# Dividing by the softmax sum ahead of the f16 split instead of behind the PV product, in a fused attention and two-MLP kernel

## The chip, the cores and the metric

The kernel runs on one core of one Trainium2 chip. The metric is the device time of one execution in microseconds. An execution is timed from outside, so its time is a little longer than the span between the first and the last instruction in the profile.

## What is computed

The input is q, k and v of 4 batches and 8 heads, 576 positions, 64 channels. For each head, the scores are `q k^T / 8`; scores lower than the row's maximum less `tau` are dropped; the rest goes through a softmax, whose denominator is the sum of the kept exponentials plus 1e-9; and the result multiplies v. The heads are laid side by side, which gives x of 2304 rows and 512 columns. The first MLP is `g(x @ w_in) @ w_out` with `g(h) = P(h) / Q(h)`, a cubic over a quadratic, and 2048 hidden columns. The second is `((x @ w1) * (x @ w2)) @ w3 @ w_out2` with 1024 columns. Everything is wanted in fp32.

## The kernel before

**Split numbers.** Most products run on f16 pairs: a number is written as hi + lo, and a product is three matmuls (hi hi, hi lo, lo hi). P and V are split too: the transposed P carries hi and lo in 9 blocks of 128 rows, V has 9 hi and 5 lo blocks, which gives the 14 steps of `pv` for each of two heads. Scores are fp32 matmuls. Weights arrive as 64-bit numbers. Three integer operations on VectorE (`conv_w`, L692, L695, L698) turn each tile of 128 x 512 into fp32, its squares give a scale, and `split_w` makes hi by a scaled copy and lo in PSUM by two products (L748 in fp32, L749) and a copy out. The product w3 w_out2 is formed once (`w_product`, L945).

**Attention.** One unit of work is (b, c, u): batch, pair of heads, and u = 0 for query blocks 0 and 1, u = 1 for blocks 2, 3 and 4 (block 4 holds 64 rows of both heads). For each block, `qk` makes scores of two heads in PSUM (tag S, two slots), `top` takes the row maximum on VectorE (L516), `thr` the threshold, and `exp` works in one of two ways: by ScalarE in two passes (L539, L544, the second summing rows into `su`), or by one pass of ScalarE (L537) and a select-and-sum on VectorE (L542). `p_hi` casts p to f16, `p_lo` subtracts, `p_t` transposes the pair by DMA (L596). Behind the last block of a unit, `recip` makes the reciprocals of 4 or 5 sums (L557, L558) and splits them into f16 hi and lo (L560, L561). `spread` multiplies them on TensorE with a small diagonal matrix `spot` (L574), so that the reciprocal of each query row stands along the free axis in PSUM; it is copied to SBUF (tile R). `pv` adds its 28 matmuls into the same PSUM bank (tag h), and `x_split` or `x_tail` multiplies that by R on VectorE (L620, L634), casts to f16 and subtracts.

**The order.** The kernel is written as a list of events (functions above, each a generator of one to five steps). A long constant string, ORDER, names for each step in turn the event's number, the engine where there is a choice (a, p or v: ScalarE, GpSimd, VectorE), and after dots the slots of the buffers that the step takes. The code issues the steps in that order, so the order within each engine's queue, and in the DMA queue of SyncE, is written out by hand. The first part of ORDER interleaves batch 0's attention with all weight work; after the last `split_w` come attention of batches 1 to 3, the first MLP (`h_product`, L824, and `y_product`, L888) and the second (`ab_product`, L995, and `o_product`, L1024).

**Setup.** Before all else `setup` issues three small loads (tau, and the coefficients a and b), fills constants on GpSimd, and works out a few scalars on ScalarE and VectorE.

Of the kernel before, what the change touches and what calls it, by code (L numbers as in the profile page):

```python
# [10 lines left out]
F32 = mybir.dt.float32  # L11
# [25 lines left out]
123.5 79v 53 125.4 102v.8 104p 123a 125a 156.0.1 36.6 106.1 127v.7 36 140.1 129p 159.0 36 43.7
30.0 161 43 131 163v.1 43 165.2.2 134v.5 167.8 165v 136p 59.2 167v 182.0.1 138 32.8 39.9 32 39 32
39 72.0 53 184.1 81.1 186 188p.2 190.4 175v.7 169p.3 53 177v 192.1 171v 190a 179.0 74.10 192a
219.0.1 55v.11 74 57.0 61.12 74 83a.2.2 221.2 62.0 80.1 61 83 80 61 116.1 207.2 99.2 223 66.0  # L40
64.13 225v.0 64 227.0.5 64 66 227v 76.0 232a.8 66 230.2 200p.7 202v 204 234v 230v 101.14 66 118.15
101 118 244.0.1 78.16 101 78 112.2 246.3 78 248 103.0 80 118 250p.1 252.1 215.5.7 85.1 194a.6
238p.0 240v 252a 196p 255.2 80 255a 105.17 105 263a.4 269.0 217p 82a.18 68v.19 107.1 281 105 265v
89.0 107 114.20 87.21 114 87 107 114 87 602.2 107 627.1 91.22 91 91 93.0 148.0 283.0.1 605.23 605
93 605 285.0 622.2 286 93 288a.2 290.1.2 150a.3.3 93 290a 150 624.24 608.0 630.25 624 95v.26 624
142.0 144 630 143.2 142v.1 630 610.27 128.1 610 173.1 146 610 594.0 146p 146v 166.0 242.2 594
130.28 145.29 130 594 109v.30 198 257a.3 130 145 613.1 259v 120.1 145 168.31 135.2 147.1 613 168
267 292.1 168 292a 613 299a.0 294v.6 151.0 295v 301p 613 304.0.1 615a.32 122.33 122 122 137.34
632.1 158.1 124.0 306.1 308 137 632 310p.0 314.2 137 314a 174.2 153.35 594 153 321a.1 277.7.4 153
323p 205.0 326.1 597a.36 126.0 328.2 312.5 632 132.0 330p.1 176.37 312a 160.38 176 133 632 155.0  # L50
160 176 160 189.2 635v.39 279p 181.1 157.1 206.40 139.0 315v.2 206 141 149 162.0 317v 178.1 164
206 170.0 191.41 212.0 149 355 172 180 191 110.0 191 180 220.2 183.42 183 183 214.43 197.1 185.1
214 187.0 214 209.1 211 222.44 228.0 209a.0 222 222 235.2 224.0 199.45 193.1 199 303.1 195 213 199
213a 70.1 229.46 213p 216.1 278.1 351.5.0 229 218.1 226 229 201.1 208.0 237.47 203 237 210 618.1
237 600.0 210 305.0 239.1 372.2 271.0 231.0 236.0 280.48 233 271a.1 280 241 353a 97.0 280 324 84.1
241 638.0 243 243 640 249v.49 256a.50 291.1 426.0 245p.0 253a.51 426 253.0 426 258v.52 272a.53
260a.54 274a.55 426 307.56 256.1 426 266p.0 251a.1 261 332.8 253v 332v 357.0.1 256a 307 339.1 307
247v.10 284.0 264v.12 268v.13 264.0 374.16 359.3 360 374 362a.2 273 364.2.1 374 366.3 287.14 311.2
364a 287 247.1 366a 287 275 264a 318.0 379.0.1 247v 275a 275v 251.0 380.0 373p.4 382 249.1 375p
251a 384a.0 260.0 249v 313.17 254a.21 276a.22 254.1 368v.3 260v 369p 254a 293.20 371.0 388.1 446.1  # L60
270v.23 293 388a 297.2 320.27 428.0 262a.3 293 320 428 331.1 313 386.3 320 270.0 313 430.0 325.0
338.2 386a 333p.6 432 272.1 319 270v 335p 400.1 432 272v 274.0 445 402.1 334.4 258.1 404a.1 274a
334 266.0 334 258a 365.1 446 266v 340.5 327.2 268.1 340 448.1 327 448.1 262.0 340 395a.8 450 430.0
358.2 397p 430.0 262v 450 406.7 337.2 346.0 348.1 346a.0 327 406a 435v 298.0 448.1 413.2 447.0.1
268a 377.2 452p 350 437 511.1 437 350p 449.2 455 350p 451 455 341.0 342 439.0 511 341a.1 344.0
361.24 344a 367.15 361 464.0 453v.2 344p 454.0.1 361 398 464 439 454a 367 352.2 439 457.1 513.0
367 457 345.1 515 458p.6 439p 515 457 441.0 316.0 343.0 460v 336.0 457v 462.1 322.0 347.6 300.8
296.1 347 363.0 354.25 347 309.1 354 378.1 349.0 407v.2 442.4.8 329.1 354 466.1 300 429.2 289.0
409p 468 468 411.1 456.6 456a 469.0.1 300 466.1 381.7 444v 356.0 389v.7 381 668.0 302.0 391p 370.0
282.0 471.3 393 376.0 472 466.0 381 474v.0 383.0 470v 425.1 478.0 385 385.0 473 385 482.0 478v  # L70
419a.9 387p.1 473 405v.29 390v.38 485a.3 421v.41 394a.33 392v.34 419.0 475.0 476.2 427.1.0 487p
476v 463a.7 390.1 433.1 419v 480p.0 410a.28 276.0 465p 390a 394.1 481p 276v 482 394v 483 475 392.0
# [1180 lines left out]
```

## Time and profile before

| what | value |
|---|---|
| median of 3 runs | 1107.4 us (1105.36 to 1110.74) |
| the profiled execution's own time | 1106.88 us |
| span in the profile | 1105.1 us |
| instructions | 16168 |
| TensorE busy | 997.3 us |
| VectorE busy | 869.7 us |
| ScalarE busy | 599.9 us |
| GpSimd busy | 330.9 us |

Busy time is the union of an engine's instructions: neighbours overlap a little at their ends, so a count times a mean is somewhat more than the busy time. Line numbers (L574) are those of the kernel before. PE is the matmul side of TensorE, PEld its weight load, DVE VectorE, ACT ScalarE, POOL GpSimd, SP SyncE; "SPq" is the DMA queue of SyncE.

### The profile page before, as it was taken

The page shows a single profiled execution, that of the slowest core. Times are in us where ns is not written, and L with a number is a line of the kernel's source. Part 1 is how long each engine was busy: PE and PEld are TensorE (multiplying, and loading weights), DVE is VectorE, ACT ScalarE, POOL GpSimd, SP SyncE. Part 2 cuts the span into 40 slices and gives each one's busy share as a digit, 9 for nine tenths or more (in the row PEclk, how much of TensorE's full clock was granted, in tenths as well). Part 3 has the DMA queues.
Part 4 walks back from the last instruction along what each step waited for, and adds up shares of the span by engine and source line. Part 5 has one row for each costly group of instructions (what it writes and reads, how often), then busy time and mean ns, then how long its engine had stood idle before and what let it go on. Part 6 is the DMA issues. An engine that isn't in the chain of part 4 may idle for free. (4 is left out here: it accounts for less than half of the span.)

```text
span 1105.1 us, 16168 instructions
## 1 busy us (share of the span) xinstructions
PE 997.3 (90%) x5599; PEld 480.3 (43%) x5604; DVE 869.7 (79%) x1756; ACT 599.9 (54%) x1118; POOL 330.9 (30%) x350
## 2 busy tenths in 40 slices
PE   3588769398789989999999999999999999999997
PEld 1334334143344445454444445454454454544443
DVE  5887888989897689889879977979778757775731
ACT  3341466777455377664677555885755434443430
POOL 2120213241131243342143354353233234321211
PEclk9889979698999999999999999999999999999999
DMA  8867787647675665768565678674675526622323
GB/s 235 218 206 210 218 208 200 175 99 192 146 196 148 129 118 115 166 131 186 110 136 116 148 140 169 134 174 85 146 146 97 112 47 132 114 58 48 58 48 86
DMA packets 334626, 154.70 MB, mean 140 GB/s; under 512 B 307408, under 2 KB 311504, under 8 KB 334544
## 3 DMA queue, kind: packets, MB, share of 16 engines
q1 hardware_dynamic: 334544, 153.67, 61.6%
q8 instruction: 44, 0.72, 0.3%
q14 instruction: 38, 0.31, 0.1%
HBM read 70.00 MB, written 8.13 MB: 71 GB/s over the span
## 5 line engine op out<-in xcount | busy, mean ns | idle before, releaser
L888 PE MATMUL y<-wp,gt 128*128 128x512 f16 x864 | 198.6, 379 | 1.7 <-DMA gt<-gg 1.1
L824 PE MATMUL h<-wp,xp 128*128 128x512 f16 x768 | 178.9, 381 | 5.0 <-DVE U L846 2.9
L349 POOL TENSOR_TENSOR hl<-p,hl 128x576 f16<-128x576 f32 x79 | 108.3, 1373 | 139.9 <-DVE hl L337 72.5
L507 PE MATMUL S<-raw 64*128 64x288 f32 x512 | 96.9, 458 | 47.8 <-ACT p L544 25.9
L995 PE MATMUL h<-wp,yy 128*128 128x512 f16 x576 | 132.6, 379 | 5.3 <-DVE R L634 1.9
L888 PEld LDWEIGHTS <-gt 128*128 128x128 f16 x864 | 82.5, 98 | 105.5 <-issue 6.9
L516 DVE TENSOR_REDUCE m<-S 128x1 f32<-128x576 f32 x144 | 104.4, 750 | 19.6 <-PE S L507 15.9
L824 PEld LDWEIGHTS <-xp 128*128 128x128 f16 x768 | 74.1, 98 | 99.2 <-issue 14.9
L1024 PE MATMUL y<-wp,gt 128*128 128x512 f16 x432 | 99.7, 379 | 0.8 <-DMA gt<-gg 0.8
L539 ACT ACTIVATE S<-S,th 128x576 f32<-128x576 f32 x97 | 67.7, 710 | 53.4 <-POOL th L356 33.7
L995 PEld LDWEIGHTS <-yy 128*128 128x128 f16 x624 | 59.4, 98 | 82.2 <-issue 12.0
L832 ACT ACTIVATE U<-h,cf 128x512 f32<-128x512 f32 x72 | 55.8, 777 | 67.1 <-PE h L824 42.4
L507 PEld LDWEIGHTS S<-raw 64*128 64x128 f32 x512 | 53.8, 198 | 88.1 <-ACT p L544 33.9
L349 POOL TENSOR_TENSOR A<-A,r 128x512 f32<-128x512 f32 x41 | 52.5, 1281 | 95.6 <-ACT r L839 95.5
L349 POOL TENSOR_TENSOR gg<-A,r 128x512 f16<-128x512 f32 x33 | 46.3, 1403 | 111.1 <-DVE A L867 76.8
L863 DVE SCALAR_TENSOR_TENSOR gg<-U,cf,r 128x512 f16<-128x512 f32 x72 | 59.1, 824 | 22.6 <-ACT r L856 15.6
L844 DVE SCALAR_TENSOR_TENSOR U<-h,cf,U 128x512 f32<-128x512 f32 x72 | 53.7, 746 | 28.1 <-ACT r L839 18.5
L544 ACT ACTIVATE p<-S,xy 128x576 f32<-128x576 f32 x97 | 71.6, 742 | 6.3 <-POOL hl L349 3.5
L748 PE MATMUL y<-cw,dg 128*128 128x512 f32 x112 | 64.1, 656 | 11.6 <-DVE gg L346 4.3
L945 PE MATMUL h<-cw 128*128 128x512 f32 x128 | 63.6, 652 | 6.5 <-DVE cw L698 2.9
L854 ACT ACTIVATE r<-A,lnb 128x512 f32<-128x512 f32 x72 | 51.8, 723 | 31.8 <-POOL A L349 23.8
L1024 PEld LDWEIGHTS <-gt 128*128 128x128 f16 x432 | 41.2, 98 | 52.1 <-issue 2.3
(199 smaller groups left out, 1697.3 us busy)
## 6 DMA issues: line engine op xcount, KB each, us to landing
rw<-in_moe_w_dram SPq DMA_DIRECT2D x32, 512.0 KB, 4.0
rw<-in_moe_w_out_dram SPq DMA_DIRECT2D x24, 512.0 KB, 4.6
raw<-in_k_dram SPq DMA_DIRECT2D x32, 288.0 KB, 3.3
wr<-in_v_dram SPq DMA_DIRECT2D x16, 576.0 KB, 4.9
rw<-in_moe_w_in_dram SPq DMA_DIRECT2D x16, 512.0 KB, 4.3
wr<-in_v_dram SPq DMA_DIRECT2D x16, 320.0 KB, 3.4
out_dram<-A SPq DMA_DIRECT2D x16, 256.0 KB, 2.5
d_y<-x SPq DMA_DIRECT2D x13, 256.0 KB, 2.3
```

Of the source, the lines that this page charges most:

```text
L349: (nc.gpsimd if eng[0] == "p" else nc.vector).tensor_tensor(o, x, y, op=op)
L507: nc.tensor.matmul(t[s][:, half, :HS], x[r, o:o + 128], y[r, keys], start=True, stop=True)
L516: nc.vector.tensor_reduce(st["m", b, c, blk][:, s:s + 1], t[:, :, :HS], axis=AX.XY, op=ALU.max, negate=True)
L539: nc.scalar.activation(t, t, AF.Prelu, bias=th, alpha=BIG)
L544: nc.scalar.activation(x, t, AF.Exp, bias=xy[:, 0:1], accum_out=su)
L748: nc.tensor.matmul(y, st["dg", dg], r, start=True, stop=False)
L824: nc.tensor.matmul(t, x[:, y, c, o:o + 128], w[:, a, :], start=c + i == 0, stop=c == KD - 1 and i == 2)
L863: stt(p[:, 0, :], u, cf[:, 3:4], r, ALU.add, ALU.mult)
L888: nc.tensor.matmul(st["y", n], x[:, 4 * a + j, :], w[:, y, :], start=f + j + i == 0, stop=f == 3 and j == 3 and i == 2)
L945: nc.tensor.matmul(t, st["cw", ("w3", m, j // 4)][:, o:o + 128], st["cw", ("wo2", j)], start=j == 0, stop=j == 7)
L995: nc.tensor.matmul(t, x[:, 4 * y + c, :], w[:, a, :], start=c + i == 0, stop=c == KD - 1 and i == 2)
L1024: nc.tensor.matmul(st["o", n], x[:, 4 * a + j, :], w[:, y, :], start=hf + j + i == 0, stop=hf == 1 and j == 3 and i == 2)
```

## The change

1. `recip` runs once for each block instead of once for each unit: (sum + 1e-9) x 2^-14 on any of three engines, then a reciprocal on VectorE. No f16 split of it. `spread`, `spot` and R go.
2. p is multiplied by the reciprocal ahead of its split. For head 0 of a block this is an extra pass over p in place (`p_norm`); for head 1 it is folded into the two steps of the split: `p_hi` gets a scale, and `p_lo` becomes one scalar-tensor-tensor operation, which only VectorE does in this code.
3. `x_split` and `x_tail` read PSUM directly: a copy scaled by 2^-14, and a scalar-tensor-tensor subtraction. The multiplication by R goes.
4. `setup` is cut into four events. `limits` (tau) and `powers` (a and b) hold the small loads, `diagonals` the two fills of 128 x 128. The new ORDER issues them as tokens 0, 1, 3, 2, then 6 (the first load of v).
5. ORDER is new throughout. The first loads are, before: tau, a, b, two weight tiles (512 KB each), v (320 KB), q, k; after: tau, a, b, two of v, one weight tile, q, k, and q, k of the next pair.
6. `su` has 8 buffers of 2 columns instead of 3 of 5; R and rr go.

Counted in the two ORDER strings, with the engine letters:

| step | whole order, before | whole order, after | up to the last split_w, before | up to the last split_w, after |
|---|---|---|---|---|
| exp, second step | 97 a, 47 v | 84 a, 60 v | 35 a, 11 v | 25 a, 21 v |
| recip | 32 of 4 VectorE instructions | 80: 40 a, 21 p, 19 v, and 80 reciprocals | 10 | 25: 14 a, 6 p, 5 v |
| p_norm | none | 36 a, 11 p, 33 v | none | 16 a, 2 p, 7 v |
| p_hi | 49 a, 33 p, 62 v | 66 a, 38 p, 40 v | 14 a, 12 p, 18 v | 20 a, 9 p, 13 v |
| p_lo | 79 p, 65 v | 47 p, 33 v, 64 fused on v | 23 p, 21 v | 15 p, 8 v, 19 fused on v |
| copy of spread to R | 26 a, 22 v | none | 8 a, 4 v | none |
| x_split, x_tail | 48 products, 96 further steps | 48 scaled copies, 48 subtractions | 12 units | 12 units |
| split_w, last copy | 34 a, 22 v | 23 a, 33 v | 34 a, 22 v | 23 a, 33 v |

Up to that point the new order also holds one more `qk` block and two more half steps of `ab_product`. The other events are the same, with some engine letters changed.

```diff
 ORDER = """
-0 45.0 49.1 1.2 12.0.1 47.0 47 47 3.0 51.1 51 51 2.0.0 13p 7.1 26.2 23.0.1 4.1 14.0 25.0 8.0 27
+0 1 3 2 6.0 4.1 49.2 15.0.1 22.2.3 5.0.0 7.1 53.1 29.0 51.0 51 16a 51 26.0.1 10.2 24a 28.0 30 55.1
...
-        R=2, m=4, th=3, su=3, rr=3, vs=2, sc=4, cf=6, xl=1,
+        m=4, th=3, su=8, vs=2, sc=4, cf=6, xl=1,
...
     def setup():
         nc.scalar.preload_act_table_set("natural_log_exp_and_others")
-        nc.sync.dma_start(out=tau_t, in_=tau.rearrange("(o c) -> o c", o=1).to_broadcast([128, 1]))
-        nc.sync.dma_start(out=pa, in_=ca.rearrange("(o c) -> o c", o=1).to_broadcast([128, 4]))
-        nc.sync.dma_start(out=bb, in_=cb.rearrange("(o c) -> o c", o=1).to_broadcast([128, 2]))
...
-        nc.gpsimd.memset(spot, 0.0)
-        nc.gpsimd.affine_select(out=spot, in_=spot, compare_op=ALU.not_equal, fill=2.0**-10,
-                                base=0, pattern=[[-1, 128]], channel_multiplier=1)
...
+        nc.vector.memset(xy[:, 1:2], 1e-9 * 2.0**-14)
+        nc.gpsimd.memset(qp, 0.0)
+
+    def limits():
+        nc.sync.dma_start(out=tau_t, in_=tau.rearrange("(o c) -> o c", o=1).to_broadcast([128, 1]))
...
-    def recip(b, c, u):
-
-        n = 5 if u else 4
-        su = st.pop(("su", b, c, u))[:, :n]
-        nc.vector.tensor_scalar(su, su, 1e-9, None, op0=ALU.add)
+    def recip(b, c, blk):
+
+        n = 2 if blk < 4 else 1
+        su = st["su", b, c, blk][:, :n]
+        small(su, su, 1e-9, 2.0**-14, xy[:, 1:2])
+        yield
         nc.vector.reciprocal(su, su)
-        t = st["rr", b, c, u] = T("rr", [128, 2, 5], F16)
-        nc.vector.tensor_scalar(t[:, 0, :n], su, 1024.0, None, op0=ALU.mult)
-        stt(t[:, 1, :n], su, 1024.0, t[:, 0, :n], ALU.mult, ALU.subtract)
-
-    def spread(b, c, u):
...
+
+    def p_norm(b, c, blk):
+        p = st["p", b, c, blk, 0]
+        copy(p, p, st["su", b, c, blk][:, 0:1])
 
     def p_hi(b, c, blk, s):
         hl = T("G", [128, 2 * S], F16, name="hl")
-        copy(hl[:, 0:S], st["p", b, c, blk, s])
+        copy(hl[:, 0:S], st["p", b, c, blk, s], st["su", b, c, blk][:, 1:2] if s else None)
         st["hl", b, c, blk, s] = hl
 
     def p_lo(b, c, blk, s):
-        hl = st["hl", b, c, blk, s]
-        rest(hl[:, S:2 * S], st.pop(("p", b, c, blk, s)), hl[:, 0:S])
+        hl, p = st["hl", b, c, blk, s], st.pop(("p", b, c, blk, s))
+        rest(hl[:, S:2 * S], p, hl[:, 0:S], st["su", b, c, blk][:, 1:2] if s else None)
...
-        t, y, p = st.pop(("pv", b, c, u)), st.pop(("R", b, c, u)), st["xp", b, u]
-        nc.vector.tensor_tensor(y, t[:, :256], y, op=ALU.mult)
-        yield
-        copy(p[:, 0, c, :], y)
-        yield
-        rest(p[:, 1, c, :], y, p[:, 0, c, :])
+        t, p = st.pop(("pv", b, c, u)), st["xp", b, u]
+        copy(p[:, 0, c, :], t[:, :256], 2.0**-14)
+        yield
+        rest(p[:, 1, c, :], t[:, :256], p[:, 0, c, :], 2.0**-14)
...
             for s in range(n):
                 at(exp, b, c, blk, s)
+            at(recip, b, c, blk)
+            at(p_norm, b, c, blk)
...
-    at(setup)
+    for fn in (setup, limits, diagonals, powers):
+        at(fn)
```

## Rows read from the trace of the kernel before

**Rows 1.** The page: clock granted to TensorE in 40 equal slices, in tenths.

```profile
PEclk9889979698999999999999999999999999999999
```

**Rows 2.** L337 by form: min/median/max ns, first and last start us.

```profile
L337 DVE CAST wp<-y x22: 676/684/693, 157.2 to 354.2; 128x512 f16<-128x512 f32 x22
...
L337 DVE CAST hl<-p x62: 446/454/1531, 24.6 to 946.1; 128x576 f16<-128x576 f32 x62
```

**Rows 3.** Windows, whole engines: us, busy (count), clock, DMA share, GB/s.

```profile
0.00:357.00 357.00, 269.57 (x1189) 126.81 (x1196) 299.91 (x645) 188.28 (x375) 83.34 (x98) 0.90 0.70 188
357.00:1105.00 748.00, 727.77 (x4414) 353.49 (x4410) 569.83 (x1111) 411.62 (x744) 247.55 (x252) 1.00 0.58 117
```

**Rows 4.** Waits, 28 to 357 us, SP's DMA queue: us, times, longest.

```profile
SPq L686 <- DVE cw L698: 62.4, 33, 4.9
```

**Rows 5.** The waits of PE in the same window.

```profile
PE S L507 <- ACT p L544: 21.2, 7, 13.2
```

**Rows 6.** Windows of L574 (spread): PE and PEld busy, clock, DMA share.

```profile
0.00:357.00 357.00, 4.97 (x80) 3.33 (x80) 0.90 0.70 188
357.00:1105.00 748.00, 12.89 (x240) 7.89 (x240) 1.00 0.58 117
```

**Rows 7.** The chain that ended last: start us, us, what.

```profile
788.52 1.29 PE h L824 x6
789.81 0.34 PE h L574 x8
790.16 1.53 PE h L611 x28
791.68 1.17 PE S L507 x8
```

**Rows 8.** Groups by form: busy us, mean ns of one, idle before, releasers.

```profile
L349 POOL TENSOR_TENSOR hl<-p,hl 128x576 f16<-128x576 f32 x79 | 108.3, 1373 | 139.9 <-DVE hl L337 72.5 <-ACT hl L333 58.6 <-issue 4.0
...
L349 DVE TENSOR_TENSOR hl<-p,hl 128x576 f16<-128x576 f32 x65 | 51.0, 784 | 5.0 <-ACT hl L333 2.1 <-POOL hl L337 1.9 <-DMA wr<-in_v_dram 0.8
...
L542 DVE SCALAR_TENSOR_TENSOR p<-S,th,p 128x576 f32<-128x576 f32 x47 | 37.6, 811 | 7.8 <-ACT p L537 7.3 <-POOL th L356 0.3
...
L346 DVE SCALAR_TENSOR_TENSOR vl<-wr,vs,vh 128x640 f16<-128x640 f32 x16 | 14.3, 904 | 2.3 <-ACT vh L335 2.3
...
L620 DVE TENSOR_TENSOR R<-h,R 128x256 f32<-128x256 f32 x32 | 13.4, 419 | 3.0 <-ACT R L333 2.3 <-PE h L611 0.7
...
L356 DVE TENSOR_SCALAR th<-m,c 128x2 f32<-128x2 f32 x24 | 6.5, 271 | 0.2
...
L339 POOL TENSOR_SCALAR wp<-cw,wsc 128x512 f16<-128x512 f32 x3 | 4.7, 1562 | 0.0
```

**Rows 9.** Window 0 to 357 us of L557 alone: DVE busy (count).

```profile
0.00:357.00 357.00, 3.23 (x10) 0.90 0.70 188
```

**Rows 10.** The same window of L561 alone.

```profile
0.00:357.00 357.00, 3.92 (x10) 0.90 0.70 188
```

**Rows 11.** The tile su: instructions of recip, min/median/max ns.

```profile
L557 DVE TENSOR_SCALAR su<-su x32: 153/170/1282, 24.9 to 947.7; 128x4 f32<-128x4 f32 x16, 128x5 f32<-128x5 f32 x16
L558 DVE RECIPROCAL su<-su x32: 177/184/192, 25.1 to 948.0; 128x4 f32<-128x4 f32 x16, 128x5 f32<-128x5 f32 x16
L560 DVE TENSOR_SCALAR rr<-su x32: 169/172/1199, 25.4 to 948.2; 128x4 f16<-128x4 f32 x16, 128x5 f16<-128x5 f32 x16
```

**Rows 12.** Windows, whole engines, two stretches dense in VectorE work.

```profile
414.00:552.00 138.00, 134.50 (x905) 67.49 (x904) 122.76 (x260) 86.16 (x164) 43.90 (x46) 1.00 0.68 142
552.00:690.00 138.00, 134.41 (x857) 66.52 (x855) 115.56 (x224) 85.69 (x158) 61.26 (x63) 1.00 0.70 142
```

**Rows 13.** Timeline of the start: start us, us, engine, line, idle before.

```profile
3.54 0.43 SPq L446 DMA_DIRECT2D raw<-in_q_dram  x1
...
7.38 0.42 DVE L692 TENSOR_SCALAR cw<-rw 128x512 int32<-128x512 int32 x1
...
9.91 1.20 POOL L339 TENSOR_SCALAR raw<-raw,flag 128x256 f32<-128x256 f32 x1 [7.29 <-DMA raw<-in_q_dram]
...
11.16 2.29 PE L507 MATMUL S<-raw 64*128 64x288 f32 x8 [11.16 <-POOL raw L339]
```

More of the change, by code (lines that the diff above doesn't have):

```diff
@@ L37 @@
[L37 to L48, printed above, removed]
@@ new lines @@
+1207a.7 1201v 1457.1 1083.1 1203a.1 1159 1295a.2.2 1204p 1218 1241.0 1091.0 1243 1206 1220v
+1245p.1 1091 1083 1209 1457 1083 1295 1210 1094.0 1066 1094.1 1083v 1160.1 1094.0 1461 1221p.5
+1452 1086.1 1247.1.8 1097 1099p 1247v 1461p.0 1229.1 1102 1097 1223p 1102 1113.0 1461p 1231v
+1224.0 1248.4 1248v 1231 1264.0.1 1250p 1464.0 1250 1105.1 1088 1252v 1266.1 1259p.1 1236.7.3
+1254a.2 1268 1088 1270v.0 1271.2.6 1466 1255p 1273.5 1271a 1113 1238p 1257.2 1273a 1105 1226.1
+1116.1 1275v 1261 1116.0 1300.0.1 1275 1116.1 1228v 1263.1 1105 1466 1162a.3.3 1228 1122p 1302.3
@@ L375, in tile_attention_mlps @@
     d1, b1, unit = c4[:, 0:1], c4[:, 1:2], c4[:, 2:3]
-    xy = cst.tile([128, 1], F32, name="xy")
+    xy = cst.tile([128, 2], F32, name="xy")
     ident = cst.tile([128, 128], F32, name="ident")
@@ L384, in tile_attention_mlps @@
     onesh = cst.tile([128, 128], BF16, name="onesh")
-    spot = cst.tile([128, 128], F16, name="spot")
     qp = cst.tile([128, 128], F32, name="qp")
@@ L413, in setup, with powers @@
                                     pattern=[[-1, 128]], channel_multiplier=1)
+    def powers():
+        nc.sync.dma_start(out=pa, in_=ca.rearrange("(o c) -> o c", o=1).to_broadcast([128, 4]))
+        nc.sync.dma_start(out=bb, in_=cb.rearrange("(o c) -> o c", o=1).to_broadcast([128, 2]))
         nc.scalar.activation(aa, pa, AF.Abs)
@@ L527, in exp @@
     def exp(b, c, blk, s):
-        u = min(blk // 2, 1)
-        if (u, s) == (0, 0) and blk == 0 or (blk, s) == (2, 0):
-            st["su", b, c, u] = T("su", [128, 5])
+        if s == 0:
+            st["su", b, c, blk] = T("su", [128, 2])
         p = T("G", [128, S], name="p")
-        x, k = p.rearrange("p (j c) -> p j c", j=2), 2 * (blk - 2 * u) + s
-        su, th = st["su", b, c, u][:, k:k + 1], st["th", b, c, blk][:, s:s + 1]
+        x = p.rearrange("p (j c) -> p j c", j=2)
+        su, th = st["su", b, c, blk][:, s:s + 1], st["th", b, c, blk][:, s:s + 1]
         t, m = st["S", b, c, blk][s][:, :, :HS], st["m", b, c, blk][:, s:s + 1]
@@ L628, in x_tail @@
     def x_tail(b, c):
-        t, y = st.pop(("pv", b, c, 2)), st.pop(("R", b, c, 2))
+        t = st.pop(("pv", b, c, 2))
         if b % 2 == 0 and c == 0:
@@ L633, in x_tail @@
         p = st["xl", b // 2][:, :, c, 64 * (b % 2):64 * (b % 2) + 64]
-        nc.vector.tensor_tensor(y, t[:, :64], y, op=ALU.mult)
+        copy(p[:, 0], t[:, :64], 2.0**-14)
         yield
-        copy(p[:, 0], y)
-        yield
-        rest(p[:, 1], y, p[:, 0])
+        rest(p[:, 1], t[:, :64], p[:, 0], 2.0**-14)
         if b % 2 and c == KD - 1:
@@ L657, in attention @@
                 at(p_t, b, c, blk, s)
-        at(recip, b, c, u)
         if u:
-            at(spread, b, c, 2)
             at(pv, b, c, 2)
             at(x_tail, b, c)
-        at(spread, b, c, u)
         at(pv, b, c, u)
```

487 lines of the change are left out of this document (241 added, 246 removed).

## The prediction

> **What bounds the kernel now.** I read the clock row of the page first: the slices in which TensorE is granted less than full speed all lie in the first quarter of the span [rows 1]. That suggests two regimes, and the last copy of a weight split, at 354 us [rows 2], shows where to cut. So the second view is the windows cut at 357 us [rows 3]. The reader should see that behind 357 us TensorE is busy 727.8 of 748 us at a granted clock of 1.00: this part is bound by matmuls, and 20 us is all that a better feed could give. Ahead of 357 us TensorE is busy only 269.6 us, at a mean clock of 0.90, while VectorE is busy 299.9 of 357 us, ScalarE 188.3 and GpSimd 83.3. VectorE is the fullest engine there, and the DMA queue confirms it: the weight loads wait 62.4 us in total for the last step of `conv_w` to free a buffer [rows 4]. It isn't a hard bound, because 57 us of VectorE stay idle; TensorE's own longest wait there is for the exponentials of the block before, which free PSUM for the next scores [rows 5]. I therefore price TensorE behind 357 us, and VectorE ahead of it.
>
> **TensorE's saving.** The L574 matmuls take 17.9 us of TensorE: 4.97 us ahead of the cut and 12.89 us behind it, 240 instructions for 12 pairs of heads [rows 6]. Behind the cut they lie on the chain that sets the end, 0.34 us for a group of eight, directly ahead of the 1.53 us of `pv` [rows 7]. Nothing hides them there, so all 12.9 us come off. The 4.97 us ahead of the cut lie where TensorE has 87 us idle; I don't count them as such. But the new order has, by the last weight split, one block of scores and two half steps of `ab_product` more behind it than the old one. On the chain a half step, six matmuls, takes 1.29 us and a block of scores 1.17 us [rows 7], so 3.7 us of later work are done in the early part in place of the spreads. What is left for TensorE behind the cut falls by 12.9 + 3.7 = 16.6 us. This assumes that the early part ends at the same time, which is the next step.
>
> **VectorE's early part.** Counts are those of the two orders up to the last `split_w`; durations are those of the rows. The select form of `exp` is used 10 times more: 10 x 0.811 = +8.1 us [rows 8]. The last copies of the weight split go from 22 to 33: 11 x 0.684 = +7.5 us [rows 2]. `p_lo`: 21 subtractions of 0.784 become 8 of them and 19 fused ones; the nearest fused operation is 0.904 us for 640 columns, or 0.81 for 576 [rows 8], together +5.2 us. `p_norm`: 7 passes. The trace shows no fp32 to fp32 pass of 576 columns; from below it is the cast at 0.454 us [rows 2], from above GpSimd's 1.56 us for 512 columns [rows 8]. On VectorE the cast is the nearer: +3.2 us. `p_hi` loses 5 casts: -2.3 us. `recip`: ten old ones took 3.23 us at L557 and 3.92 at L561 [rows 9, 10], and 10 x (0.184 + 0.172) at the two between [rows 11], 10.7 us; the new ones are 5 x 0.271 [rows 8] and 25 x 0.184 [rows 11], 6.0 us: -4.7 us. `x_split`, `x_tail` and the copies to R, 12 units: the product (0.419 for 256 columns [rows 8]) goes, as do four copies to R and nine further steps on VectorE; 12 subtractions and a copy come, each as long as the product, since they too read PSUM: about -4 us. Engine letters changed elsewhere take about 2.8 us off. The sum is +10 us of VectorE, on 300.
>
> How much of that reaches the end of the early part? Nothing, if it fits into the 57 idle us; 10 x 357/300 = 12 us, if the part keeps its ratio of busy time. VectorE waits little and is fed by loads that wait for it, so I'm nearer the second end: +7 us.
>
> **The part behind the cut, VectorE.** With the same prices on the whole order, the densest 100 us of TensorE in the old order carry 100 us of VectorE, and in the new one 104 us. Such a stretch measured 122.8 us of VectorE in 138, with TensorE still at 134.5 [rows 12], so the prices, which count overlapping ends twice, are about a tenth high, and four per cent more should still fit. ScalarE gets most of `p_norm` and has 52 of 138 us free there. I take +2 us, between 0 and +4. GpSimd has 94 us free in the same stretch: its 21 long scaled passes are hidden there by the distance between a block and its `pv`. If that cover were gone, each would cost its 1.56 us or more.
>
> **The start.** The constants don't in fact go behind the first loads: `limits` and `powers`, with their three DMAs, stand in the order ahead of the first load of v, as before. What moves is one weight tile, to behind v and q: 192 KB less ahead of q, which SP issued at 3.54 us and which GpSimd began to scale at 9.91; ScalarE now scales it, and the first matmul waited for that, at 11.16 us [rows 13]. In return the first `conv_w`, at 7.38 us, gets its tile later. Two pairs of q and k are now queued ahead of the second weight tile. Between -1.5 and +1 us; I take 0. The wait of recip's second step on its first, possibly on another engine, holds VectorE's queue at that place; what is queued behind are weight conversions and maxima, and it is in the 7 us above.
>
> **Sum.** 1106.9 (the profiled execution's own time) - 16.6 + 7 + 2 = 1099.3. That execution is 0.5 us below the median of the runs, well within their spread, so I forecast 1099 us.
>
> **A rule weighed.** VectorE's short tensor-scalar operations show a median of 0.170 us and a maximum of 1.28, while the reciprocal never exceeds 0.192 [rows 11]; the cast of p shows 0.454 and 1.53 [rows 2]. The Trainium skill, SBUF — State Buffer, section "Who interferes with whom", says that copies, casts and tensor-scalar operations on VectorE can take a port pair shared with GpSimd, and that the later of the two then stands still for the whole instruction of the other. The trace agrees in which instructions have the long tail. What it would do here is the last rival.
>
> **The rivals.**
> The early cost is hidden. VectorE's 10 us go into its idle 57, and the dense stretch costs nothing: 1106.9 - 16.6 - 1 = 1089. For it: TensorE's longest early waits are for exponentials [rows 5], which the normalization doesn't delay. Against it: the loads wait for VectorE [rows 4].
> Given back. The early part grows by the full 12 us, the dense stretch by 4 and the start by 1: 1106.9 - 16.6 + 17 = 1107. For it: VectorE is the fullest engine in both places.
> Slower. The normalization lengthens the way of each early block from its exponentials to its transposed P: threshold-sized step 0.27, reciprocal 0.18, `p_norm` 0.45 or more, 0.9 us at least, and about 1.2 with the waits between. If the early part is a chain through its 25 blocks rather than VectorE's sum, it grows by 30 us, and the time is 1106.9 - 16.6 + 30 + 2 = 1122. This decides from 0.66 us a block for no gain (16.6/25), and 0.9 for slower by half a per cent. Against it: scores wait for the exponentials alone, and the order keeps other work between a block and its `pv`.
> VectorE held. If each of the seven early `p_norm` passes on VectorE is held like the longest L557 (1.28 - 0.17 = 1.1 us), 7.8 us are added to the forecast: 1107. Against it: the median shows that most aren't held, and GpSimd has 32 fewer subtractions of 1.37 us [rows 8] to hold them with.
>
> **How the numbers follow.** Forecast 0.47, hidden 0.15, given back 0.15, slower 0.17, held 0.06. The forecast's own range is 1093 to 1105 (early part between +1 and +12, start and dense stretch at their ends in part). Half a per cent, 5.5 us, is about what a measurement of this kernel can tell from no change: faster is below 1101.9, slower above 1112.9. Of the forecast about 0.37 lies below 1101.9, and with the hidden case that is 0.52; 0.10 of it, given back and held make 0.31; slower 0.17. The range reaches from the hidden case's 1088 to 1113; the slower case is left outside.
>
> **What would show it.** No matmuls from a diagonal of 2^-10, TensorE's busy time lower by about 18 us; behind the last weight split TensorE 97% busy for some 731 us; that split's end at about 364 us, with VectorE busy about 310 us until then. If it ends near 357, the hidden case holds; if past 375, the slower one, and the scores' matmuls should then wait for more than the 21 us seen. If TensorE's idle time behind it is well above 20 us, the dense stretch was mis-sized. The forecast is wrong above all if the early part isn't ruled by VectorE's sum.

## The result, and the profile after

The changed kernel takes 1091.2 us, median of four runs (1090.44 to 1095.06), against 1109.07 for the kernel before in the same rounds: a ratio of 0.985, interval 0.981 to 0.989. A second, longer set of runs gave 1091.67 against 1106.94, 0.986 (0.984 to 0.989). The forecast of 1099 us was 8 us too long: the result lies below the forecast's own range (1093 to 1105) and only inside the wider one that takes in the hidden case, whose 1089 is nearer. Of the profiled executions, 1106.88 us became 1090.44: 16.4 us less, where 7.6 were forecast.

First the page of the changed kernel: busy time of each engine, and the clock granted in 40 slices.

```profile
PE 985.8 (91%) x5284; PEld 469.6 (43%) x5284; DVE 882.7 (81%) x1755; ACT 626.9 (58%) x1159; POOL 327.2 (30%) x325
...
PEclk9979979788999999999999999999999999999999
```

The low clock still stands in the first quarter alone, as in [rows 1]: the two parts are still there. The windows of the changed kernel at the same cut as [rows 3] (TensorE, its weight loads, VectorE, ScalarE, GpSimd, then clock, DMA share, GB/s):

```profile
0.00:357.00 357.00, 269.59 (x1137) 123.89 (x1138) 309.62 (x661) 197.87 (x384) 92.97 (x95) 0.91 0.71 189
357.00:1088.70 731.70, 716.20 (x4149) 345.73 (x4147) 573.12 (x1094) 429.03 (x776) 234.23 (x230) 1.00 0.60 119
```

Behind 357 us there are 731.7 us left, and VectorE is busy 309.6 us ahead of it: both are close to the figures that the prediction named (731 and 310). What it had wrong is where the last weight split ends. Its last copy starts at 352.8 us on ScalarE, the last on VectorE at 349.6, where the one before started at 354.2 [rows 2] and 364 was forecast. L336 and L340 are the new lines of the copies (minimum, median and maximum in ns, first and last start in us):

```profile
L336 ACT ACTIVATE wp<-y x23: 575/597/598, 153.2 to 352.8; 128x512 f16<-128x512 f32 x23
```

```profile
L340 DVE CAST wp<-y x33: 667/682/693, 155.3 to 349.6; 128x512 f16<-128x512 f32 x33
```

So from here on I cut each kernel at its own split: at the start of the last matmul that computes a split's remainder, 353.4 us before and 352.4 us after. The windows of the kernel before at that cut:

```profile
0.00:353.40 353.40, 265.97 (x1170) 125.06 (x1176) 298.38 (x642) 186.22 (x371) 80.46 (x96) 0.90 0.70 188
353.40:1105.10 751.70, 731.37 (x4430) 355.24 (x4428) 571.37 (x1115) 413.68 (x747) 250.43 (x255) 1.00 0.58 117
```

And those of the changed kernel:

```profile
0.00:352.40 352.40, 264.99 (x1115) 121.78 (x1116) 307.05 (x657) 194.34 (x377) 88.71 (x92) 0.91 0.72 191
352.40:1088.70 736.30, 720.80 (x4170) 347.84 (x4168) 575.70 (x1099) 432.57 (x782) 238.49 (x234) 1.00 0.60 119
```

The whole gain lies behind the split: 751.7 - 736.3 = 15.4 us, of which TensorE's busy time gives 731.4 - 720.8 = 10.6 and its idle time the rest (751.7 - 731.4 = 20.3 became 736.3 - 720.8 = 15.5). The early part is 1.0 us shorter, although VectorE does 8.7 us more in it. A second profile of the same kernel cuts elsewhere:

```profile
0.00:354.50 354.50, 264.32 (x1111) 121.58 (x1117) 307.09 (x657) 194.38 (x377) 88.50 (x92) 0.91 0.71 190
354.50:1089.20 734.70, 719.62 (x4170) 347.45 (x4168) 576.16 (x1099) 432.46 (x782) 238.41 (x234) 1.00 0.60 119
```

So 2 us of such a cut mean nothing, and the runs below show more scatter than that. Seven profiles of the new order with these 4170 matmuls behind the cut and no work added there have 718.6 to 721.2 us of TensorE behind it, in 732.0 to 736.6 us; two profiles of the old order with 4430 matmuls there have 731.4 and 735.6. Of the kernel before there is one profile only.

The waits of the early part (28 to 357 us, changed kernel), first the DMA queue, then TensorE: total, times, longest.

```profile
SPq L668 <- DVE cw L680: 67.9, 37, 4.5
```

```profile
PE S L506 <- DVE p L545: 13.4, 1, 13.4
PE h L696 <- ACT sq L687: 11.5, 7, 3.6
PE S L511 <- DVE p L545: 10.2, 4, 5.0
PE y L730 <- ACT wp L336: 7.2, 5, 2.7
PE S L511 <- ACT p L547: 5.5, 1, 5.5
```

The weight loads wait for VectorE a little longer than in [rows 4] (67.9 against 62.4 us), and the scores wait for the exponentials as in [rows 5]: 13.4 + 10.2 + 5.5 = 29.1 us, against 21.2 + 7.0 = 28.2 in the kernel before, whose second wait is for the exponentials that VectorE finishes:

```profile
PE S L507 <- DVE p L542: 7.0, 2, 6.5
```

None of TensorE's long waits is for a transposed P. What the normalization costs on each engine is shown by the tile of the sums:

```profile
L562 DVE RECIPROCAL su<-su x80: 147/156/167, 17.3 to 931.8; 128x2 f32<-128x2 f32 x64, 128x1 f32<-128x1 f32 x16
L349 DVE SCALAR_TENSOR_TENSOR hl<-p,su,hl x64: 790/810/1825, 18.3 to 928.2; 128x576 f16<-128x576 f32 x64
...
L338 ACT ACTIVATE p<-p,su x36: 759/775/800, 35.2 to 932.6; 128x576 f32<-128x576 f32 x36
...
L342 DVE TENSOR_SCALAR p<-p,su x33: 501/514/1161, 17.5 to 918.9; 128x576 f32<-128x576 f32 x33
...
L342 POOL TENSOR_SCALAR p<-p,su x11: 1723/1725/2811, 179.1 to 925.9; 128x576 f32<-128x576 f32 x11
```

One pass of `p_norm` is 0.514 us on VectorE (0.454 was assumed from the cast [rows 2]), 0.775 on ScalarE and 1.725 on GpSimd (medians). The fused subtraction is 0.810, as its nearest row, scaled to 576 columns, said [rows 8].

The start of the changed kernel:

```profile
3.54 0.44 SPq L450 DMA_DIRECT2D raw<-in_q_dram  x1
...
8.72 0.43 DVE L674 TENSOR_SCALAR cw<-rw 128x512 int32<-128x512 int32 x1 [1.53 <-DMA rw<-in_moe_w_dram]
...
9.06 0.51 ACT L338 ACTIVATE raw<-raw,flag 128x256 f32<-128x256 f32 x1
...
9.93 2.29 PE L511 MATMUL S<-raw 64*128 64x288 f32 x8 [9.93 <-DMA raw<-in_k_dram]
```

Against [rows 13], the first scores start 1.23 us sooner and the first `conv_w` 1.34 us later.

### The profile page after: what moved, and what is told of

It reads as the page before. It is cut to its first block, busy times and chain, and to the rows that moved or that the text cites. A ratio compares the mean times of both kernels' runs of the same rounds, so it can differ in the third digit from the quotient of the medians.

```text
span 1088.7 us, 15602 instructions
## 1 busy us (share of the span) xinstructions
PE 985.8 (91%) x5284; PEld 469.6 (43%) x5284; DVE 882.7 (81%) x1755; ACT 626.9 (58%) x1159; POOL 327.2 (30%) x325
## 5 line engine op out<-in xcount | busy, mean ns | idle before, releaser
L806 PEld LDWEIGHTS <-xp 128*128 128x128 f16 x768 | 74.5, 99 | 99.1 <-issue 15.5
L352 POOL TENSOR_TENSOR hl<-p,hl 128x576 f16<-128x576 f32 x47 | 66.8, 1421 | 108.5 <-ACT hl L336 58.3
L511 PEld LDWEIGHTS S<-raw 64*128 64x128 f32 x512 | 53.6, 198 | 75.4 <-issue 31.6
L730 PE MATMUL y<-cw,dg 128*128 128x512 f32 x112 | 66.7, 680 | 14.1 <-ACT wp L336 7.2
L826 DVE SCALAR_TENSOR_TENSOR U<-h,cf,U 128x512 f32<-128x512 f32 x72 | 53.4, 745 | 31.7 <-ACT r L821 18.7
L542 ACT ACTIVATE S<-S,th 128x576 f32<-128x576 f32 x84 | 58.1, 710 | 20.5 <-POOL th L359 13.1
L845 DVE SCALAR_TENSOR_TENSOR gg<-U,cf,r 128x512 f16<-128x512 f32 x72 | 54.2, 757 | 19.0 <-DMA gt<-gg 10.1
L547 ACT ACTIVATE p<-S,xy 128x576 f32<-128x576 f32 x84 | 62.1, 743 | 5.8 <-DMA pL<-hl 4.8
L927 PE MATMUL h<-cw 128*128 128x512 f32 x128 | 60.6, 626 | 2.5 <-ACT cw L336 1.4
```

Source lines behind the costliest of these rows:

```text
L352: (nc.gpsimd if eng[0] == "p" else nc.vector).tensor_tensor(o, x, y, op=op)
L511: nc.tensor.matmul(t[s][:, half, :HS], x[r, o:o + 128], y[r, keys], start=True, stop=True)
L542: nc.scalar.activation(t, t, AF.Prelu, bias=th, alpha=BIG)
L547: nc.scalar.activation(x, t, AF.Exp, bias=xy[:, 0:1], accum_out=su)
L730: nc.tensor.matmul(y, st["dg", dg], r, start=True, stop=False)
L806: nc.tensor.matmul(t, x[:, y, c, o:o + 128], w[:, a, :], start=c + i == 0, stop=c == KD - 1 and i == 2)
```

## The experiments

Two things were open: what the spread matmuls had really been worth (their recorded time, or less, by overlap), and why the early part did not grow (because VectorE's sum does not rule it, or because something was given back there). Ratios are to the kernel before in the same rounds; the changed kernel's own is 0.986. "Cut" is the last split, as above, and "behind" what lies from there to the end.

**The matmuls put back.** The new order, with matmuls of the number and shapes of the old spread ahead of each `pv`, from constants (of bf16, where the old ones were f16).

```diff
         vh, vl = st["v", b, c]
+        for i in range(2 if u < 2 else 1):
+            for a in range(2):
+                for h in range(2):
+                    ...
+                    nc.tensor.matmul(d, onesh[k, 0:64], onesh[k, k], start=a == 0, stop=a == 1)
```

> The changed kernel with the 320 small matmuls of spread put back on TensorE ahead of each pv: same shapes and count as before, operands constant, results in a part of the PSUM bank that nobody reads; all else as changed. Theory A (TensorE alone sets the time behind the last weight split, so the removed matmuls are the gain): slower than the changed kernel by 12.9 us, the busy time of these matmuls behind the cut in the kernel before, up to 16.5 with the gaps around them, which gives 1104 to 1108 us against a changed kernel of 1091. Theory B (the gain comes from the new order, not from the matmuls): slower by at most 5 us.

Measured: 1094.12 us, 0.9888 (0.9871 to 0.9904): by the ratios only some 3 us above the changed kernel. The windows of these matmuls alone (TensorE, weight loads) and of the whole:

```profile
356.90:1093.80 736.90, 12.88 (x240) 7.83 (x240) 1.00 0.60 119
```

```profile
356.90:1093.80 736.90, 724.30 (x4410) 353.29 (x4408) 572.27 (x1099) 432.48 (x782) 238.62 (x234) 1.00 0.60 119
```

By the record they are busy 12.88 us behind the cut, as before [rows 6]. TensorE's busy time rises by 3.5 us (720.8 to 724.3), its idle time falls by 2.9, and the part is 0.6 us longer, within the scatter of that part; the cut comes at 356.9, 2.4 to 4.5 later. A line's busy time is not what its presence costs. Part of it is overlap, which the timeline shows (start, us, what):

```profile
613.00 0.41 PE L600 MATMUL h<-onesh 128*64 128x128 bf16 x8
613.25 1.15 PE L606 MATMUL h<-pT,vh 128*64 128x256 f16 x18
```

A group of eight is recorded as 0.41 us, but `pv` starts 0.25 us after it did. So theory A is refuted for the matmuls by themselves.

**The matmuls taken out of the old order.** The kernel before, with no spread matmuls, and R filled with ones.

```diff
-        for i in range(2 if u < 2 else 1):
...
-                    nc.tensor.matmul(d, w.to_broadcast([k.stop - k.start, 64]), spot[k, k],
-                                     start=a == 0, stop=a == 1)
...
-        copy(y, t[:, n:2 * n])
+        copy(y, unit.to_broadcast([128, n]))
```

> The kernel before with its old order, but without the matmuls of spread; R is filled with ones by the same copies, so x isn't divided by the sums. Theory A: faster than before by 12.9 to 16.5 us, ratio 0.985 to 0.988, although order, setup and VectorE's work are the old ones. Theory B: at most 5 us faster, ratio 0.995 or more.

Measured: 1086.99 us, 0.9822 (0.9803 to 0.9841), 20 us less. Its windows:

```profile
0.00:345.60 345.60, 256.51 (x1091) 119.93 (x1096) 297.74 (x642) 185.19 (x370) 83.48 (x97) 0.92 0.72 192
345.60:1083.90 738.30, 721.70 (x4190) 349.19 (x4188) 571.22 (x1115) 413.00 (x748) 248.94 (x254) 1.00 0.59 119
```

Here the part behind the cut loses 751.7 - 738.3 = 13.4 us: 9.7 of TensorE's busy time and 3.7 of its idle time. And the early part, where VectorE does the same work as before (297.7 us), ends 7.8 us sooner. The time fell by more than theory A allowed, in the old order.

The two experiments differ in more than the order. The matmuls that I put back wait for nothing, and nobody waits for them; the old spread worked on the reciprocals, and its result was copied to R. In the kernel before, by its profile, these copies wait for `pv`, which writes the same PSUM bank, 16.1 us on VectorE and 20.7 on ScalarE in all (total, times, longest):

```profile
DVE R L337 <- PE h L611: 16.1, 14, 2.7
ACT R L333 <- PE h L611: 20.7, 11, 4.2
```

This run takes away these waits together with the matmuls, since its copies read a constant.

**The same in batch 0 alone.** The loop of the spread runs only where `b` is not 0, and R of batch 0 is filled with ones.

```diff
-        for i in range(2 if u < 2 else 1):
+        for i in range((2 if u < 2 else 1) if b else 0):
```

> The kernel before without the matmuls of spread in batch 0 alone (R is ones there, so batch 0 isn't divided by its sums); batches 1 to 3 as before. Without them everywhere the early part ended 7.8 us sooner and the rest took 13.4 us less. Theory E (the 4.97 us of spread ahead of the cut and the waits of TensorE in front of them, 3.0 us, lie on the path of the early part): the last weight split ends at about 346 us instead of 353, the rest is unchanged, and the time falls by 7 to 8 us. Theory F (TensorE's idle time takes the early spreads up; the earlier end had another reason): the split stays at 353 and the time falls by 2 us at most.

Measured: 1104.44 us, 0.9969 (0.9954 to 0.9985), 3.4 us less. Its windows:

```profile
0.00:347.00 347.00, 261.64 (x1095) 121.20 (x1096) 298.04 (x642) 185.39 (x370) 82.17 (x97) 0.91 0.71 191
347.00:1102.30 755.30, 735.61 (x4430) 356.63 (x4428) 571.32 (x1115) 414.20 (x748) 248.40 (x254) 0.99 0.58 117
```

The cut comes at 347.0, 6.4 us sooner, as theory E said, but the time falls by half of that: the part behind the cut is 3.6 us longer (755.3). So batch 0's 4.97 us of spread [rows 6], which lie where TensorE is idle a quarter of the time, do matter for the early end, with the waits and copies that go with them. Whether the other half is lost behind the cut or is scatter of single profiles (4.6 us in the new order) isn't shown; the times, with their interval, give 1.7 to 5.1 us.

**The matmuls put back elsewhere.** The same number, behind the scores of a pair's last block, into unused columns of S.

```diff
             st.pop(("qk", b, c, u))
+            for i in range(2 if blk == 1 else 3):
+                ...
+                        nc.tensor.matmul(d, onesh[k, 0:64], onesh[k, k], start=a == 0, stop=a == 1)
```

> The changed kernel with the same 320 dummy matmuls as in the run in which they stood directly ahead of pv, now directly behind the scores of a unit's last block, apart from pv, into unused columns of the scores' PSUM banks. Theory G (what such a group costs depends on its neighbour: beside pv, whose matmuls have the same size of stationary operand, 0.1 us a group; apart, 0.34 us): the part behind the cut is 8 to 10 us longer than in the changed kernel, against 0.6 us beside pv. Theory H (it doesn't depend on the place): 0.6 to 3 us longer, as beside pv.

Measured: 1096.74 us, 0.99 (0.9876 to 0.9923), by the ratios 4 us above the changed kernel. Behind the cut:

```profile
354.90:1095.50 740.60, 728.13 (x4386) 353.35 (x4384) 574.10 (x1098) 432.13 (x782) 239.56 (x234) 1.00 0.59 118
```

That is 4.3 us more than the changed kernel, between the two theories' figures, with 7.3 us more of TensorE's busy time. Of the added matmuls 216 lie there, recorded as 10.85 us, not 240. And the place brings waits of its own: VectorE's row maxima wait 9.1 us in the whole kernel for these matmuls, which stand in the scores' banks. So it isn't shown that the matmuls themselves cost more away from `pv`.

**Three sets of them.** As in the first experiment, three times.

```diff
+        for i in (0, 1) * 3 if u < 2 else (0,) * 3:
```

> The changed kernel with three times the matmuls of spread ahead of each pv (960, operands constant, nobody reads the results). One set, which on TensorE takes 0.21 us where eight stand together and 0.1 where four do, 6.3 us behind the cut, made the part behind the cut only 0.6 us longer and the kernel about 4 us slower. Theory J (TensorE is the bound behind the cut, but 3 us of its idle time there is slack that the first set used up): each further set comes in full, 12.6 us behind the cut and 3 us ahead of it, so 16 to 20 us slower than the changed kernel. Theory K (the small matmuls beside pv cost next to nothing): 4 to 8 us slower.

Measured: 1100.54 us, 0.9943 (0.9921 to 0.9966), 9 us above the changed kernel. Its windows behind the cut, of these matmuls and of the whole:

```profile
350.90:1096.70 745.80, 25.12 (x720) 20.07 (x720) 1.00 0.58 117
```

```profile
350.90:1096.70 745.80, 735.61 (x4890) 365.99 (x4888) 573.24 (x1099) 433.66 (x782) 237.35 (x234) 1.00 0.58 117
```

Against one set, two more add 735.6 - 724.3 = 11.3 us of busy time and 745.8 - 736.9 = 8.9 us behind the cut, 4.5 us a set. By the ratios, which rest on several runs each, one set costs 3.1 us and three cost 9.2: some 3 us a set, with no sign that the first is cheaper. That is nearer the lower expectation, and a quarter of the 12.9 us of the record. Ahead of the cut the three sets are busy 9.02 us by the record, and still the cut comes at 350.9, no later than the changed kernel's: the early part isn't lengthened by the matmuls' time as such. With one set it came at 356.9, so single cuts can differ by some 6 us for no reason that these runs show.

**VectorE's early load raised.** Two reductions of 512 columns, 0.68 us each, behind each reciprocal of batch 0: 40 in all.

```diff
         nc.vector.reciprocal(su, su)
+        for _ in range(2 if b == 0 else 0):
+            nc.vector.reduce_max(spare[:, 512:513], spare[:, 0:512], axis=AX.X)
```

> The changed kernel with two more reductions over 512 columns of a spare constant tile on VectorE behind each reciprocal of batch 0: 40 instructions of some 0.68 us, 27 us in all, in the early part where VectorE has 47 us idle. Theory C (VectorE's sum rules the early part): slower by 27 x 357/310 = 31 us. Theory A (idle time takes it up): slower by 5 us at most, with the last weight split within 5 us of its place.

Measured: 1105.81 us, 0.999 (0.9975 to 1.0005). Its early window:

```profile
0.00:371.00 371.00, 264.84 (x1110) 122.36 (x1116) 332.10 (x697) 194.51 (x377) 84.66 (x93) 0.90 0.68 181
```

25 us more of VectorE (332.1 against 307.1) move the cut by 16.5 to 18.6 us (to 371.0, from 354.5 or 352.4), and the time by 14: about 0.7 us for each us, the share of 7 in 10 that the forecast took. Neither theory's figure (31 and 5 us) was met.

**VectorE's early load lowered.** 24 early steps given to ScalarE by their letters in the order: the 7 `p_norm` and 17 last copies of `split_w`. The first and the last of them:

```diff
-... 40v ... 68v ... 929v ... 807v
+... 40a ... 68a ... 929a ... 807a
```

> The changed kernel with 24 steps of the early part moved from VectorE to ScalarE by their letters in the order: the 7 passes of p_norm (0.54 us each on VectorE, 0.77 on ScalarE) and 17 of the 33 last copies of the weight split (0.68 and 0.59). Takes 15 us off VectorE ahead of the cut and adds 15 us to ScalarE, which has 158 us idle there. Theory C (VectorE's sum reaches the early part's end with the slope of 0.69 that the run with more VectorE work showed): 10 us faster than the changed kernel. Theory I (ScalarE's queue then holds exponentials behind copies that wait for TensorE): 0 to 5 us faster, or slower.

Measured: 1090.91 us, 0.9845 (0.9817 to 0.9872). Its early window:

```profile
0.00:352.10 352.10, 261.78 (x1115) 120.53 (x1116) 295.05 (x633) 207.25 (x401) 86.78 (x91) 0.91 0.72 191
```

VectorE is 12.0 us shorter, ScalarE 12.9 longer, and the cut (352.1) and the time stay where they were. Theory C's 10 us are refuted for this move. It doesn't show that less work on VectorE is worth nothing, since ScalarE took the steps over: TensorE's waits for ScalarE's squares and copies of the weight split rise there from 11.5 + 7.2 = 18.7 us to

```profile
PE h L691 <- ACT sq L682: 13.8, 9, 3.6
PE y L725 <- ACT wp L331: 9.1, 8, 2.7
```

which is 22.9. Work moved to another engine isn't work taken away; no run takes early work off VectorE alone.

**No normalization.** `p_norm` does nothing; all other steps stay.

```diff
-        p = st["p", b, c, blk, 0]
-        copy(p, p, st["su", b, c, blk][:, 0:1])
+        pass
```

> The changed kernel without p_norm, so head 0 of each block isn't divided by its sum. Takes 36 passes off ScalarE, 11 off GpSimd and 33 off VectorE (17.9 us busy there), and one link from the way from exponentials to transposed P. Theory A (these passes are hidden in idle time): same as the changed kernel within 3 us. Theory C (VectorE's sum still rules the early part, as forecast): the early part ends about 4 us sooner (7 passes of 0.54 us on VectorE) and the time falls by 4 us. Theory D (the chain of each early block rules): 25 blocks by 0.5 us or more, 12 us faster.

Measured: 1086.34 us, 0.9828 (0.9806 to 0.9849): the 80 passes cost some 4 us, and the interval touches the changed kernel's. The cut comes at 349.8, against 352.4 and 354.5, with 2.9 us less of VectorE ahead of it and 11.3 less of ScalarE. Theory D is refuted; theories A (3 us) and C (4 us) can't be told apart. The new order without its normalization and the old order without its spread take the same time, 1086.3 and 1087.0.

**VectorE's load raised in the dense part.** One reduction behind each reciprocal of batches 1 to 3, 60 in all.

```diff
         nc.vector.reciprocal(su, su)
+        if b:
+            nc.vector.reduce_max(spare[:, 512:513], spare[:, 0:512], axis=AX.X)
```

> The changed kernel with one more reduction over 512 columns on VectorE behind each reciprocal of batches 1 to 3: 60 instructions of 0.66 us, 40 us of VectorE, nearly all behind the cut, where VectorE has 160 us idle. Theory J (TensorE alone bounds that part): 0 to 3 us slower. Theory L (the dense stretch from about 400 to 700 us, where VectorE is busy 90 per cent, is bound by VectorE too, as the 2 us of the forecast suppose): 6 to 15 us slower, with TensorE's idle time up in that stretch.

Measured: 1104.13 us, 0.9972 (0.9956 to 0.9988), 12 us above the changed kernel. Its part behind the cut, two stretches of it, and the same two of the changed kernel:

```profile
354.80:1104.00 749.20, 723.95 (x4170) 348.97 (x4168) 607.34 (x1155) 433.31 (x782) 237.40 (x235) 1.00 0.56 117
```

```profile
400.00:540.00 140.00, 131.56 (x828) 65.20 (x828) 128.28 (x260) 96.07 (x181) 56.23 (x51) 0.99 0.69 143
540.00:680.00 140.00, 135.59 (x771) 65.48 (x771) 128.08 (x244) 87.49 (x159) 51.12 (x50) 1.00 0.68 142
```

```profile
400.00:540.00 140.00, 135.56 (x859) 66.77 (x857) 127.05 (x257) 99.65 (x186) 59.62 (x53) 1.00 0.74 149
540.00:680.00 140.00, 139.29 (x833) 69.17 (x833) 123.90 (x252) 90.93 (x168) 55.09 (x56) 1.00 0.73 149
```

VectorE stays at 128 of 140 us, little above the 127 and 124 that the changed kernel has there; what gives way is TensorE, from 135.6 to 131.6 and from 139.3 to 135.6. Behind the cut VectorE has 31.6 us more, the part is 749.2 - 736.3 = 12.9 us longer, and TensorE's idle time in it rises from 15.5 to 25.3. So, as theory L has it, the dense part is not bound by TensorE alone: each us of VectorE costs 0.4. TensorE's busy time also rises by 3.2 us here, with not one matmul more: a rise of that size, such as the first set's 3.5, needn't be the added matmuls' own time.

**The constants really behind the loads.** In the order, the tokens of `limits` (1), `powers` (3) and `diagonals` (2) after the first loads.

```diff
-0 1 3 2 6.0 4.1 49.2 15.0.1 22.2.3 5.0.0 ...
+0 6.0 4.1 49.2 15.0.1 1 22.2.3 3 2 5.0.0 ...
```

> The changed kernel with the constants in fact behind the first loads: the two loads of v, the weight tile and the first q and k are issued first, then tau, then the second q and k, then the coefficients and the diagonals. Theory: the first three loads start 1.4 us sooner (three issues of 0.47 us less ahead of them), and tau, 1.7 us later in the queue, still lands ahead of q; the scores start 0.5 to 1.4 us sooner and the time falls by 0 to 1.5 us. Rival: the scaling of q waits for tau behind 1.1 MB of loads, and the time grows by 1 to 3 us.

Measured: 1095.39 us, 0.9877 (0.985 to 0.9904), not told apart from the changed kernel's 0.986. Its part behind the cut (735.0 us) and the cut itself (354.9) are those of the changed kernel. At the start it is the rival that came true: tau is used from 8.62 us on, where it was used from 3.31, and the first scores start 2.75 us later than the changed kernel's:

```profile
12.68 1.81 PE L511 MATMUL S<-raw 64*128 64x288 f32 x6 [12.68 <-ACT raw L338]
```

**Normalization folded into the split.** For the 33 blocks whose subtraction runs on VectorE, the sum's reciprocal is applied in the split of the first head instead of ahead of it; 14 `p_hi` go from GpSimd to ScalarE.

```diff
-        copy(hl[:, 0:S], st["p", b, c, blk, s], st["su", b, c, blk][:, 1:2] if s else None)
+        copy(hl[:, 0:S], st["p", b, c, blk, s], scale_of(b, c, blk, s))
...
-        rest(hl[:, S:2 * S], p, hl[:, 0:S], st["su", b, c, blk][:, 1:2] if s else None)
+        rest(hl[:, S:2 * S], p, hl[:, 0:S], scale_of(b, c, blk, s))
```

> A variant that computes the whole reference: in the 33 blocks in which VectorE does head 0's subtraction, the extra pass p_norm goes, and head 0 is scaled inside its split as head 1 is (a scaled p_hi, on ScalarE in 14 blocks where GpSimd cast it, and the fused subtraction). It takes 33 passes away: 15 on ScalarE (0.77 us), 12 on VectorE (0.54), 6 on GpSimd (1.96); it adds 0.05 to 0.1 us to each split step. Leaving all 80 passes out made the kernel some 3 us faster. Theory A (the passes are hidden): within 1 us of the changed kernel. Theory C: 1 to 3 us faster.

Measured: 1092.53 us, 0.986 (0.9833 to 0.9888): no gain. With at most 4 us to be had from all of `p_norm`, a third of it can't be seen.

**The changed kernel once more**, beside the last group of runs, for the cut's scatter.

> The changed kernel itself once more, beside the kernel before on the chip of this group of runs, so that differences of 3 to 6 us can be told: all theories expect a ratio of 0.982 to 0.988.

Measured: 1091.67 us, 0.9863 (0.9837 to 0.9889); cut 354.5, behind it 734.7 us, TensorE busy 719.6.

## Why the prediction was right, and which term was mis-sized

**In short.** The sign was right. The size wasn't: 15 to 18 us came off where 8 were forecast, and the result is inside the stated range only by the part of it that belongs to the hidden case. The term that was mis-sized is the early part, +7 us forecast and about -1 measured. The largest term, TensorE's 16.6 us, came out close to the number, but not by the matmul time that it was built on, so that its fit is in part luck.

**What bounds the kernel.** The cut into two parts held: behind 357 us 731.7 us were left, where 731 was named (748 - 16.6, without the 2 us of the dense stretch). But "this part is bound by matmuls" is only nearly so. The 60 late reductions show that VectorE, at 127 of 140 us, holds it too.

**TensorE's saving** ("all 12.9 us come off", and 3.7 by the new order: 16.6). Between the cuts 15.4 us came off (17.0 by the second profile), against 14.6 forecast (16.6 less the dense stretch's 2). The size is right, its reason is not shown to be. The step "Nothing hides them there, so all 12.9 us come off" failed: put back in the new order, the same recorded 12.88 us cost some 3 us a set. In the old order the spread as a whole was worth 13.4 us there, 9.7 of them busy time and 3.7 idle, but that takes in the copies to R, which waited for `pv`. Nor do the 3.7 us of work done earlier show in full: 20 matmuls did move ahead of the cut (4190 behind it without the spread in the old order, 4170 in the new), but TensorE's busy time behind it is only 0.9 to 2.1 us below the old order's without the spread. TensorE's whole busy time fell by 997.3 - 985.8 = 11.5 us, not by the 18 that the prediction named. The Trainium skill, Trainium Kernel Development and Optimization, section "Performance Expectations", calls the busy time of matmuls a bad measure of how near a kernel is to its limit, since matmuls are pipelined. That is said of a whole kernel; here a single line shows the like, with 12.88 us of record and some 3 us of time for a set.

**VectorE's early part** (+10 us). Right: 8.7 us between the cuts, and 309.6 at 357 us. By item, the select form is 0.810 us (0.811 taken), the fused subtraction 0.810 (0.81), `p_norm` 0.514 (0.454), the reciprocal 0.156 (0.184).

**"How much of that reaches the end"** (+7 us). The slope is right for work added to it: 0.7, by the 40 reductions. Yet the end didn't move. The step that failed here is an earlier one, a term put at nothing: "The 4.97 us ahead of the cut lie where TensorE has 87 us idle; I don't count them as such." Taken out of batch 0 alone they end the early part 6.4 us sooner, out of all batches 7.8 us sooner, with VectorE's own work unchanged. So the account between the cuts is +6 for VectorE (0.7 of 8.7) and -6.4 to -7.8 for the early spread, which gives -0.4 to -1.8; -1.0 was measured, +1.1 in the second profile. By the time of the whole kernel batch 0's spread is worth less, 3.4 us. It doesn't seem to be the matmuls' own time that counted there, since three sets put back in the new order leave the cut at 350.9. Nor is it their waits in TensorE's queue: the longest two, for `cw` (1.2 us) and `r` (1.0), stand before the first matmuls of `pv` once the spread is out (1.3 and 1.0). With equal work, the earlier end means less idle time of VectorE up to the cut: 353.4 - 298.4 = 55.0 us before, 345.6 - 297.7 = 47.9 without the spread (and 352.4 - 307.1 = 45.3 in the changed kernel). In the kernel before, VectorE's waits for TensorE from 28 us to the cut include

```profile
DVE m L516 <- PE S L507: 2.9, 3, 2.2
DVE R L337 <- PE h L611: 2.8, 3, 1.1
```

and without the spread the first is 0.5 us and the second gone (four waits of the products with R, 1.7 us, stand there instead): 3.5 of the 7.1 us. ScalarE's copies to R wait there too, 9.7 us in three. So the likely way is that VectorE, the fullest engine, stood for the copies to R and for scores that came later. That it was this way, and that the two terms of +6 and -7 cancel, is an account from separate experiments on the old and the new order, each cut from one profile; no one run shows it.

**The dense stretch** (+2). With 4.3 us more of VectorE behind the cut (571.4 to 575.7) and the 0.4 measured, 1.7 us; TensorE's idle time there didn't rise above 20 us, but fell to 15.5. Without the spread the old order has 16.6, so the fall goes with the spread.

**The start** (0). As written: the constants stayed ahead, the scores came 1.2 us sooner, the first weight tile 1.3 later. Moving the constants for real gained nothing, and held up the first scores.

**The sum.** 1106.9 - 15.4 - 1.0 = 1090.5 measured, against 1106.9 - 16.6 + 7 + 2. The 8 us between forecast and result are the early part's.

**The rivals.** *Hidden*: its time (1089) was the nearest, and its sign was seen (the end near 357), but its reason, that VectorE's work falls into idle time, is refuted by the 40 reductions, which moved the end by 16.5 us or more; what paid was, as far as shown, the early spread. *Given back*: no, neither part grew. *Slower*, by a chain through 25 blocks: the early end didn't move, the scores waited 29.1 us where 28.2 was the figure before, and without `p_norm` it comes 2.6 to 4.7 us sooner, not 11 (25 x 0.45) or more. *VectorE held*: the median of `p_norm` on VectorE is 0.514 us and the longest of 33 is 1.16; the seven early ones lie between 0.508 and 0.521, so none of them was held.

**Open.** What 12 us less of VectorE would bring if no other engine took them over: what else ends with it in the early part was not isolated (the weight loads wait 64.9 and 67.9 us for `conv_w` with and without the move). Nor is it shown how the old spread's price, 20 us in the old order, divides between the matmuls, their place and the waits of the copies to R. And one rival stands: the new order was never run with the old spread as it was, with its reciprocals and its copies to R, so that what the new order by itself gives isn't known.

## What to carry to other kernels

Don't price a line of small matmuls by its busy record: if you can, put in one and then three sets of it and time that, and count apart what its readers wait for. Here the record said 12.9 us in the matmul-bound part alone, a whole set cost some 3, and taking the line out together with its readers' waits gave 20. Steps on an engine that is idle a quarter of the time are not free if others queue behind their waits: 5 us of early matmuls, taken out with their waits, brought the early part's end 6 to 8 us forward here, and the time 3. And a load moved to another engine is not a load removed: 25 us added to the fullest engine cost 17, while 12 us moved from it to the next gave nothing. Cuts read from single profiles scattered by up to 6 us, so that differences of that size want several runs.

## What the runs showed of the hardware that was not expected

240 matmuls with weights of 64 columns are recorded as 12.88 to 12.89 us busy, in the kernel before and put back in the new order, yet a set ahead of `pv` made the new kernel some 3 us longer, and three sets 9.2; a group of eight recorded as 0.41 us let the next line start after 0.25. TensorE was busy 96.8 and 99.5% of two stretches in the dense part, and still 31.6 us of added VectorE work made the part behind the cut 12.9 us longer; TensorE's own busy sum rose by 3.2 us with no matmul added. And the same `p_norm` pass of 576 columns took 0.514 us on VectorE, 0.775 on ScalarE and 1.725 on GpSimd.
